# The first loads of a fused attention and token-mixing kernel: first k tile in four parts, second k tile cast by VectorE

## The chip, the cores and the metric

The kernel runs on one core of one Trainium2 chip. That core has a matrix engine (TensorE, PE in the profile), whose weight loads are shown apart (PEld), three engines for elementwise work (VectorE is DVE, ScalarE is ACT, GpSimd is POOL) and SyncE (SP), which here only issues DMAs. Each engine has its own list of instructions; they wait for one another by semaphores. The metric is the device time of the whole kernel in microseconds, the median of several runs; lower is better.

## What is computed

Sigmoid attention over 8 batches and 12 heads (sequence 448, head size 64), and then a token-mixing layer on its output:

```python
scores = (1/sqrt(64)) * q @ k.T - log(448)      # per batch and head
attn   = sigmoid(scores)
x      = (attn @ v), heads side by side         # 8 x 448 x 768
W_tok  = (1/8) * (x @ w_q) @ (x @ w_k).T        # 448 x 448 per batch
out    = relu(W_tok @ x) @ w_out
```

All inputs and the output are f32 in DRAM; the kernel casts to bf16 for TensorE.

## The kernel before: how the work is laid out

**Groups.** The work is cut into 24 groups (`quads`, L106): one batch and four heads each. A group has a q, a k and a v tile of 128 x 896 f32 (448 KB each, loaded by one DMA, `load1`, L155). For q and k each such tile is cast to bf16 (`cast1`, L173), transposed so that the head dimension lies on the partitions, and copied into a tile `qk[n]`. For groups 0 to 3 the transpose is done by TensorE into PSUM, with a copy from PSUM behind it (`tr`, L234, or `tr_part`, L755, for group 0); later groups use VectorE's own transpose.

**Scores.** Every group has seven score steps i = 0 to 6 (`scores`, L280): four matmuls of 64 x 448 take the i-th slice of k against all of q, into two PSUM banks, and ScalarE takes the sigmoid of the 128 x 896 result (L289). So there are 168 sigmoids. Then `values` (L295) multiplies with v. The rest, the token mixing of one batch, is spread among the scores of later groups.

**Order of the work.** Nothing is reordered by a compiler: instructions stand on each engine in the order in which the program emits them. That order is the hand-written string `PLAN` (L117): each letter is one step, in order. `S` is the next score step; `q` and `k` the transposes of the next group's q and k by TensorE; `p`/`P` a value step; `F` a filler matmul of zeros (L776); `K` the second part of group 0's k (L809). The plan of before starts `FFSSFKSFSSqFSkFSFSp`.

**Casts and loads.** `ORDER` (L657) lists the loads in their order: `q1 k1 v0 q2 .k2 v1 k3 ...`. Loads go through six buffers (`ring`, `pump_loads`, L679): a load is emitted when the cast of the tile six places earlier has been emitted, and waits for it. Names without a dot are cast by GpSimd as soon as `ready` (L692) allows (`pump`, L721). Names with a dot are cast by VectorE: `cast_by_others` (L740) is called after each score step, and `cast_one` (L730) emits the cast at VectorE's place of that moment, if at least `LAG` = 9 score steps have been emitted since the load was.

**Group 0.** Its q comes by one DMA and its k by two (slices 0 to 2, `KA`, 192 KB, and slices 3 to 6, `KB`, 256 KB; L637 to L639). The prelude casts q in two parts (VectorE and ScalarE), k in two parts (both GpSimd, L746), and calls `tr_part` for q's two parts and for `KA`; the part `KB` is transposed and copied at letter `K`, so ahead of the third score step. Group 1 has kind "a": its q is transposed at letter `q`, its k at letter `k`, and then one VectorE copy takes both from PSUM (L272, 128 x 1792).

**PSUM.** The eight banks are handed out as four pairs in turn (`bank2`, L72); a score step, a `tr_part`, or a group's q and k transposes hold one pair until the copy or sigmoid that reads it is done.

Of the kernel before, what the change touches and what calls it, by code (L numbers as in the profile page):

```python
# [17 lines left out]
def kernel(  # L18
# [17 lines left out]
    P = 128  # L36
# [47 lines left out]
    def release(fb):  # L84
        if isinstance(fb, int):
            free2.append(fb)
        elif (fb[0], 1 - fb[1]) in halves:
            halves.remove((fb[0], 1 - fb[1]))
            free2.append(fb[0])
        else:  # L90
            halves.append(fb)
# [18 lines left out]
    def xt(u, j):  # L110
# [4 lines left out]


    PLAN = (  # L117
        "FFSSFKSFSSqFSkFSFSpFSpSqpPpPSPSSkFSpPSFSSabSrPSPSPXSsPSPpPSp"
        "pPpSPSXSwwSSzWWXwWSPPpSPppNSPSqkSXSSpUSPSpMpSPpPSqkSSPSpPMSP"
        "PPPSSWWXSSwWWWSPpcPSdMpSPPPSXSNSxSqkSUSpPSMppSppPSOoSMSOOqSk"  # L120
        "SoOSMrPpSppPSPSPOoSSsSOzXOSCLlLSLSLLSpPPPPcpPSSdOOSOSCNxSOSc"
        "USPPSPdprPSPPSPPsPPPSpSOPSXoSxSzooSCMLlCSLllLSPcpPSPPPPSCSOd"
        "XSSOOoSMpcpSPPPPSPSONSMYOxSpPpSpSCoodSpPPSoOSxSUSLcldllSLLPS"
        "PpSPpcpPdSoSOMSoSOSXmMrPsSpPPSPoSpOSPoSoozxSoScOSSOOOSOdNSOS"
        "USPppSMPpppPPPSpLPlSLLeppSflLOomgcOMooNOSxSoOStoSSOooeSpPdPP"
        "oPSpSPooSOfSooSSgPOoMpppSPPPOmMOSOSOSLLLlLSLSOoSOxScoOxSoSOO"
        "NdPPSPPPPSSPoOSOSOSooSxoSOSTPpSPPSPppPPMPPypMpPlLMLLyLLIxiiN"
        "IIuiIMiImmIIIOooOOOOoOOoooooo"
    )
    PLAN = "".join(PLAN)  # L130
    KIND = ["a"] + [t for t in PLAN if t in "qacer"]
# [65 lines left out]
    def transposes(ps, t16, r):  # L197

        for x, i in enumerate(range(r.start, r.stop)):
            for g in range(2):  # L200
                for h in range(2):
                    nc.tensor.transpose(
                        ps[HALF[g], h, x * NP : (x + 1) * NP], t16[HALF[h], i, g, :],
                        ident16[HALF[h], HALF[h]],
                    )
# [28 lines left out]
    def tr(n, nm, kind):  # L234
        t = "qk".index(nm)
        if kind == "s":
            return
        if kind == "r":
            qk[n] = p_qk.tile([P, 2, 2, NI, NP], BF16, tag="qk", name="qk")
            w = pq[n].rearrange("p e t i d y -> p e (t i d y)").bitcast(F32)  # L240
            for e in range(2):
                nc.vector.transpose(out=qk[n][:, e].rearrange("p t i n -> p (t i n)").bitcast(F32), in_=w[:, e])
            return
        if kind in "cdef":
            assert n in arranged
            w = pq[n].rearrange("p e t i d y -> p e (t i d y)").bitcast(F32)[:, t]
            if t == 0:
                qk[n] = p_qk.tile([P, 2, 2, NI, NP], BF16, tag="qk", name="qk")
            nc.vector.transpose(out=qk[n][:, t].rearrange("p t i n -> p (t i n)").bitcast(F32), in_=w)  # L249
            if kind in "ef":  # L250
                if t == 0:
                    moves.append((n, p_mv.tile([P, 2, 2 * S], BF16, tag="mv", name="mv")))
                nc.vector.transpose(out=moves[-1][1][:, t].bitcast(F32), in_=w)
            return
        t16 = ld.pop((nm + "16", n))
        if t == 0:
            ps_qk[n] = bank2()
        fb, _, ps = ps_qk[n]
        if kind in "abh":
            transposes_whole(ps[:, t], t16, slice(0, NI))  # L260
        else:
            transposes(ps[:, :, t * S : (t + 1) * S], t16, slice(0, NI))
        if t == 1:
            qk[n] = p_qk.tile([P, 2, 2, NI, NP], BF16, tag="qk", name="qk")
            copy = COPY["s" if kind in "jh" else "v"]
            if kind in "abh":
                copy(
                    out=qk[n].rearrange("p h t i n -> p t i h n"),
                    in_=ps[:, :, 0 : 2 * S].rearrange("p t (i h n) -> p t i h n", i=NI, h=2),
                )  # L270
            else:
                copy(  # L272
                    out=qk[n].rearrange("p h t i n -> p t h (i n)"),
                    in_=ps[:, :, 0 : 2 * S].rearrange("p h (t x) -> p t h x", t=2),
                )
            release(fb)
# [376 lines left out]
    for t in wqks:  # L653
# [1 line left out]


    ORDER = (  # L657
# [71 lines left out]

    def cast_one(e):  # L730
        todo = BY[e]
        if not (todo and todo[0] in issued and done["S"] >= issued[todo[0]] + LAG and ready(*todo[0])):
            return False
        nm, n = todo.pop(0)
        assert e == "v" or nm in "vw" or KIND[n] in "qa"
        cast_now(nm, n, e)
        pump()
        return True

    def cast_by_others():  # L740
        while cast_one("s") or cast_one("v"):
            pass

    q016 = p_c16.tile([P, NI, 2, HD], BF16, tag="q16", name="q16")
    k016 = p_c16.tile([P, NI, 2, HD], BF16, tag="k16", name="k16")
    for t16, t32, r, e in ((q016, q0, IA, "v"), (q016, q0, IB, "s"), (k016, k0, KA, "g"), (k016, k0, KB, "g")):  # L746
        COPY[e](
            out=t16[:, r].rearrange("p i b d -> p b i d"),
            in_=t32[:, :, cols(r)].rearrange("p b (i d) -> p b i d", d=HD),
        )  # L750
    cast |= {("q", 0), ("k", 0)}
    pump_loads()
    qk[0] = p_qk.tile([P, 2, 2, NI, NP], BF16, tag="qk", name="qk")

    def tr_part(nm, t16, r, e):  # L755
# [7 lines left out]

    tr_part("q", q016, IA, "v")
    tr_part("q", q016, IB, "s")
    tr_part("k", k016, KA, "v")
    used |= {("q", 0), ("k", 0)}
    pump()

    ALIKE = dict(a="q", c="q", e="q", r="q", b="k", d="k", f="k", s="k", j="k", h="k", X="x", y="x", Y="x", g="g", z="z", L="W", l="W", T="U", t="U", I="O", i="O")  # L770
    done["q"] = done["k"] = 1
    quads_r = []

    for t in PLAN:
        if t == "F":
            nc.tensor.matmul(pairs[free2[0]][:, 0], zeros[:, 0:P], zeros, start=True, stop=True)  # L776
            continue
        kind = ALIKE.get(t, t if t in "qkx" else t.upper())
        c = done[kind]
        done[kind] += 1  # L780
        tail = done["S"] == N * NI
        if t == "S":
            scores(*divmod(c, NI))
            cast_by_others()
        elif kind == "P":
            n, i = divmod(c, NI)
            values(n, i, tail, "s" if t == "p" else "v")
            if i == NI - 1:
                used.add(("v", n))
                pump()  # L790
        elif kind in "qk":
            if t in "rs":
                quads_r.append(c) if t == "r" else None
                if t == "s":
                    quadrants(c, 0)
            tr(c, kind, t)
            if t in "df":
                used.add(("q", c))
            if t not in "cers":
                used.add((kind, c))  # L800
                pump()
        elif t == "g":
            move()
        elif t == "z":
            n = quads_r.pop(0)
            quadrants(n, 1)
            used.update({("q", n), ("k", n)})
            pump()
        elif t == "K":  # L809
            tr_part("k", k016, KB, "v")  # L810
        elif kind == "x":
            tr_x(c, tail, t in "XY", "s" if t in "yY" else "v")
        elif kind == "W":
            mlp_wqk(*divmod(c, NC), tail, t in "wl", t in "Ll")
        elif kind == "C":
            for y in range(2):
                nc.sync.dma_start(out=wout16[HALF[y], NC + c, :], in_=wout16[HALF[1 - y], c, :])
        elif kind == "N":
            mlp_wkn(c)
        elif kind == "U":  # L820
            (mlp_tmp_tiled if t in "Tt" else mlp_tmp)(c, t in "ut")
        elif kind == "M":
            u, x = divmod(c, NC // 2)
            mlp_mix(u, x, t == "m", tail)
            if x == NC // 2 - 1:
                if u // 2 in TW:
                    chunks.extend((u // 2, ((u % 2, i), (u % 2, 6 - i))) for i in range(3))
                    if u % 2:
                        chunks.append((u // 2, ((0, 3), (1, 3))))
                else:  # L830
                    chunks.extend((u // 2, m, -1) for m in (range(3, NI) if u % 2 else range(3)))
        elif kind == "O":
            if (opened or chunks)[0][0] in TW:
                out_pair(t == "o")
            elif t in "Ii":
                out_halves(t == "i")
            else:
                out_chunk(t == "o", tail)
# [29 lines left out]
```

## Time and profile before

| | |
|---|---|
| median of 3 runs (lowest, highest) | 191.03 us (190.49, 191.83) |
| the profiled execution's own time | 189.1 us |
| its span in the profile | 187.0 us |
| TensorE (PE) busy | 174.7 us, 93% |
| ScalarE (ACT) busy | 163.5 us, 87% |
| VectorE (DVE) busy | 138.8 us, 74% |
| GpSimd (POOL) busy | 107.7 us, 58% |
| HBM read and written | 35.78 MB, 11.01 MB |

The span is what the profile covers, from the first instruction to the last; the own time has 2.1 us around it. The median is that of other executions. Busy time on PE counts matmuls as they overlap in the array, so a PE that is 93% busy is not at 93% of its peak. A timeline line gives start and duration in us, the engine, the line of the kernel, the operation, what is written and read, and, in brackets, how long the engine stood idle before it and what ended that.

### The profile page before, as it was taken

Reading aid. Unit: us, or ns where it says so; the run is one execution under the profiler, and the core shown is the slowest. Engines: PE = TensorE matmul, PEld = TensorE weight load, DVE = VectorE, ACT = ScalarE, POOL = GpSimd, SP = SyncE. Lnnn points to the kernel's source line nnn. Section 1 sums busy time; section 2 is a strip of 40 time slices with the busy share of each in tenths; the row PEclk is TensorE's granted clock in tenths of the full one; section 3 lists DMA queues with packets and bytes.
Section 4 is the critical chain, followed back from the end, with each engine's and each line's share of the span. In section 5 each row is a group of like instructions: output and inputs, shape, how many; then the busy total and the mean of one; then the engine's idle time right before and its main releaser. Section 6 shows DMA issues by size and latency. Waiting matters only on the chain.

```text
span 187.0 us, 8500 instructions
## 1 busy us (share of the span) xinstructions
PE 174.7 (93%) x3645; PEld 115.4 (62%) x3648; DVE 138.8 (74%) x211; ACT 163.5 (87%) x210; POOL 107.7 (58%) x145
## 2 busy tenths in 40 slices
PE   7688899989999999999999999999999999999990
PEld 7234556554555554565555776767997989786650
DVE  3234597677878999989898999979868465797810
ACT  4599999999999989999999999998999989975120
POOL 1366698991976999999999884396032910010000
PEclk9999999999999999999999999999999999999998
DMA  5999999975599989999998996984898634603485
GB/s 170 345 341 366 323 368 330 393 271 186 182 307 404 384 284 276 361 337 340 296 278 274 311 407 240 291 282 128 231 348 292 170 96 89 156 23 85 102 238 168
DMA packets 26389, 48.97 MB, mean 262 GB/s; under 512 B 4080, under 2 KB 20208, under 8 KB 26352
## 3 DMA queue, kind: packets, MB, share of 16 engines
q1 hardware_dynamic: 25952, 47.65, 78.6%
q10 hardware_dynamic: 400, 0.79, 1.2%
q8 instruction: 28, 0.46, 1.0%
q14 instruction: 9, 0.07, 0.1%
HBM read 35.78 MB, written 11.01 MB: 250 GB/s over the span
## 4 chain that ended last, share of the span: by engine, by line
PE 69%; DVE 14%; ACT 6%; DMA 4%; issue 3%; SPq 1%; POOL 1%; ACTq 0%; DVEq 0%
PE banks L284 15%; PE banks L302 13%; PE banks L497 13%; PE banks L577 11%; ACT at L289 5%; DMA k<-in_k_dram 4%; DVE qk L218 4%; PE banks L534 3%; DVE xt L311 3%; PE banks L368 3%; PE banks L412 3%; PE banks L342 2%; PE banks L325 2%; DVE mx L440 2%; DVE qk L272 2%
## 5 line engine op out<-in xcount | busy, mean ns | idle before, releaser
L289 ACT ACTIVATE at<-banks 128x896 bf16<-128x896 f32 x168 | 141.5, 927 | 5.3 <-PE banks L284 4.0
L284 PE MATMUL banks<-qk 64*64 64x448 bf16 x672 | 63.1, 359 | 3.5 <-DVE qk L272 0.9
L302 PE MATMUL banks<-at,v 64*64 64x448 bf16 x672 | 46.6, 350 | 0.2
L284 PEld LDWEIGHTS <-qk 64*64 64x64 bf16 x672 | 25.8, 105 | 24.9 <-issue 14.8
L497 PE MATMUL banks<-wout,mx 64*64 64x384 bf16 x672 | 35.5, 323 | 0.1
L188 POOL CAST v<-v 128x896 bf16<-128x896 f32 x22 | 20.4, 931 | 14.1 <-DMA v<-in_v_dram 13.0
L302 PEld LDWEIGHTS <-v 64*64 64x64 bf16 x672 | 23.1, 106 | 7.8 <-issue 1.7
L497 PEld LDWEIGHTS <-mx 64*64 64x64 bf16 x672 | 24.7, 107 | 3.3
L311 DVE CAST xt<-banks 128x896 bf16<-128x896 f32 x20 | 21.6, 1085 | 4.5 <-PE banks L302 4.2
L440 DVE TENSOR_SCALAR mx<-banks 128x1024 bf16<-128x1024 f32 (+2 forms) x21 | 21.1, 1010 | 5.2 <-PE banks L464 3.0
L577 PE MATMUL banks<-wout,mx 128*128 128x384 bf16 (+1 forms) x138 | 24.7, 320 | 0.0
L577 PEld LDWEIGHTS <-mx 128*128 128x128 bf16 x138 | 11.9, 98 | 10.5 <-issue 4.7
L178 POOL CAST qk<-k 128x896 bf16<-128x896 f32 x11 | 13.4, 1218 | 7.8 <-DVE qk L249 5.2
L178 POOL CAST qk<-q 128x896 bf16<-128x896 f32 x13 | 16.0, 1228 | 2.7 <-DVE mx L440 1.5
L249 DVE STREAM_TRANSPOSE qk<-qk 128x448 f32<-128x448 f32 x24 | 14.9, 628 | 0.0
L377 POOL COPY wq<-wqk 64x448 bf16<-64x448 bf16 x6 | 3.3, 554 | 17.4 <-DVE wqk L376 17.1
L153 POOL COPY qk<-swap 32x448 uint32<-32x448 uint32 x20 | 12.1, 606 | 1.2
L506 DVE COPY o<-banks 128x768 f32<-128x768 f32 x9 | 8.6, 952 | 5.1 <-PE banks L497 5.1
L147 POOL COPY swap<-qk 32x448 uint32<-32x448 uint32 x20 | 11.1, 554 | 1.2
L150 POOL COPY qk<-qk 32x448 uint32<-32x448 uint32 x20 | 11.1, 554 | 1.2
L606 ACT COPY o<-banks 128x384 f32<-128x384 f32 x10 | 4.8, 485 | 7.1 <-PE banks L577 4.9
L218 DVE STREAM_TRANSPOSE qk<-qk 32x448 f32<-32x448 f32 x16 | 10.2, 636 | 0.4
(89 smaller groups left out, 227.3 us busy)
## 6 DMA issues: line engine op xcount, KB each, us to landing
q<-in_q_dram SPq DMA_DIRECT2D x24, 448.0 KB, 5.8
v<-in_v_dram SPq DMA_DIRECT2D x24, 448.0 KB, 6.5
k<-in_k_dram SPq DMA_DIRECT2D x23, 448.0 KB, 6.4
out_dram<-o SPq DMA_DIRECT2D x51, 192.0 KB, 4.3
w<-in_moe_w_out_dram SPq DMA_DIRECT2D x6, 384.0 KB, 4.0
wout<-wout SPq DMA_DIRECT2D x12, 96.0 KB, 7.1
out_dram<-o ACTq DMA_DIRECT2D x3, 192.0 KB, 3.2
qk<-mv SPq DMA_DIRECT2D x8, 56.0 KB, 3.9
```

Source lines behind the costliest of these rows:

```text
L153: eng.tensor_copy(out=w[lo, 1], in_=z[lo])
L178: COPY[e](out=f[:, :, "qk".index(nm)].rearrange("p e i d y -> p e y i d"), in_=ld.pop((nm, n)).rearrange("p (y i e d) -> p e y i d", y=2, ...
L188: COPY[e](out=t16.rearrange("p i b d -> p b i d"), in_=ld.pop((nm, n)).rearrange("p b (i d) -> p b i d", i=NI),)
L218: nc.vector.transpose(out=qk[n][other : other + 32, h].rearrange("p t i n -> p (t i n)").bitcast(F32), in_=w[own : own + 32, 1 - h],)
L249: nc.vector.transpose(out=qk[n][:, t].rearrange("p t i n -> p (t i n)").bitcast(F32), in_=w)
L284: nc.tensor.matmul(sc[HALF[h], g, 0:S], qk[n][HALF[g], h, 1, i, :], qk[n][HALF[g], h, 0].rearrange("p i n -> p (i n)"), start=True, stop=True,
L289: nc.scalar.activation(at, sc[:, :, 0:S], ACTF.Sigmoid, bias=attn_bias, scale=attn_scale)
L302: nc.tensor.matmul(ps[HALF[g], h, 0:S], ld["v16", n][HALF[h], i, g, :], ats[n, i][HALF[h], g, :], start=(i == 0), stop=(i == NI - 1),)
L311: COPY[eng](out=xt(u, j)[:, :, 0:S], in_=ps[:, :, 0:S])
L440: nc.vector.tensor_scalar(dst, ps, moe_scale, 0.0, ALU.mult, ALU.max)
L497: nc.tensor.matmul(ps[HALF[x], y, 0:NB], mx[HALF[y], u, b, 64 * (i - 3 * y) : 64 * (i - 3 * y) + 64], wout16[HALF[y], slot(y, b), x * NB : ...
L577: nc.tensor.matmul(ps, mxs[w][:, 2 * S * c + m * P : 2 * S * c + (m + 1) * P], wout16[:, c, w0:w1], start=(c == 0), stop=(c == NC - 1),)
```

## The change

The parts of the change, in the order of the code:

- `PLAN` starts with one `F` in place of two, and letter `k` of group 1 comes one score step later (behind score step 6 of group 0, where it was behind 5). The rest of the plan is the same.
- `tr` for group 1 copies its q from PSUM at letter `q` and its k at letter `k`, each by a VectorE copy of 128 x 896, in place of one copy of 128 x 1792.
- `ORDER` has `.k1` for `k1`: group 1's k is cast by VectorE. For groups 0 and 1 the `LAG` of 9 score steps is dropped, so that the cast is emitted after the first score step.
- Group 0's k is cast and transposed in four parts: K1 (slice 0), K2 (slices 1, 2), K3 (slices 3, 4), K4 (slices 5, 6). GpSimd casts K1, K2 and K4, VectorE casts K3. K1 and K2 are transposed and copied in the prelude; K3 and K4 at letter `K`. The two DMAs of group 0's k stay as they are.
- The first `pump_loads()` is called ahead of the prelude's casts, and again behind them.
- One more matmul of zeros (128 x 128) stands ahead of the plan.

```diff
-        "FFSSFKSFSSqFSkFSFSpFSpSqpPpPSPSSkFSpPSFSSabSrPSPSPXSsPSPpPSp"
+        "FSSFKSFSSqFSFSkFSpFSpSqpPpPSPSSkFSpPSFSSabSrPSPSPXSsPSPpPSpp"
...
+        if n == 1:
+            if t == 0:
+                qk[n] = p_qk.tile([P, 2, 2, NI, NP], BF16, tag="qk", name="qk")
+            nc.vector.tensor_copy(
+                out=qk[n][:, :, t].rearrange("p h i n -> p h (i n)"), in_=ps[:, :, t * S : (t + 1) * S],
+            )
+            if t == 1:
+                release(fb)
+            return
...
-        "q1 k1 v0 q2 .k2 v1 k3 q3 q4 k4 v2 w0 v3 k5 k6 q5 "
+        "q1 .k1 v0 q2 .k2 v1 k3 q3 q4 k4 v2 w0 v3 k5 k6 q5 "
...
-        if not (todo and todo[0] in issued and done["S"] >= issued[todo[0]] + LAG and ready(*todo[0])):
+        if not (todo and todo[0] in issued and done["S"] >= issued[todo[0]] + (LAG if todo[0][1] > 1 else 0) and ready(*todo[0])):
...
+    pump_loads()
     q016 = p_c16.tile([P, NI, 2, HD], BF16, tag="q16", name="q16")
     k016 = p_c16.tile([P, NI, 2, HD], BF16, tag="k16", name="k16")
-    for t16, t32, r, e in ((q016, q0, IA, "v"), (q016, q0, IB, "s"), (k016, k0, KA, "g"), (k016, k0, KB, "g")):
+    K1, K2, K3, K4 = slice(0, 1), slice(1, 3), slice(3, 5), slice(5, 7)
+    for t16, t32, r, e in (
+        (q016, q0, IA, "v"), (q016, q0, IB, "s"), (k016, k0, K1, "g"), (k016, k0, K2, "g"), (k016, k0, K4, "g"),
+    ):
...
-    cast |= {("q", 0), ("k", 0)}
-    pump_loads()
...
-    tr_part("k", k016, KA, "v")
+    tr_part("k", k016, K1, "v")
+    tr_part("k", k016, K2, "v")
+    COPY["v"](
+        out=k016[:, K3].rearrange("p i b d -> p b i d"), in_=k0[:, :, cols(K3)].rearrange("p b (i d) -> p b i d", d=HD),
+    )
+    cast |= {("q", 0), ("k", 0)}
+    pump_loads()
...
+    nc.tensor.matmul(pairs[free2[0]][:, 0, 0:P], zeros[:, 0:P], zeros[:, 0:P], start=True, stop=True)
...
         elif t == "K":
-            tr_part("k", k016, KB, "v")
+            tr_part("k", k016, K3, "v")
+            tr_part("k", k016, K4, "v")
```

More of the change, by code (lines that the diff above doesn't have):

```diff
@@ L117 @@
     PLAN = (
-        "FFSSFKSFSSqFSkFSFSpFSpSqpPpPSPSSkFSpPSFSSabSrPSPSPXSsPSPpPSp"
[L119 to L128, printed above, removed]
+        "FSSFSKFSSqFSFSkFSpFSpSqpPpPSPSSkFSpPSFSSabSrPSPSPXSsPSPpPSpp"
+        "PpSPSXSwwSSzWWXwWSPPpSPppNSPSqkSXSSpUSPSpMpSPpPSqkSSPSpPMSPP"
+        "PPSSWWXSSwWWWSPpcPSdMpSPPPSXSNSxSqkSUSpPSMppSppPSOoSMSOOqSkS"
+        "oOSMrPpSppPSPSPOoSSsSOzXOSCLlLSLSLLSpPPPPcpPSSdOOSOSCNxSOScU"
+        "SPPSPdprPSPPSPPsPPPSpSOPSXoSxSzooSCMLlCSLllLSPcpPSPPPPSCSOdX"
+        "SSOOoSMpcpSPPPPSPSONSMYOxSpPpSpSCoodSpPPSoOSxSUSLcldllSLLPSP"
+        "pSPpcpPdSoSOMSoSOSXmMrPsSpPPSPoSpOSPoSoozxSoScOSSOOOSOdNSOSU"
+        "SPppSMPpppPPPSpLPlSLLeppSflLOomgcOMooNOSxSoOStoSSOooeSpPdPPo"
+        "PSpSPooSOfSooSSgPOoMpppSPPPOmMOSOSOSLLLlLSLSOoSOxScoOxSoSOON"
+        "dPPSPPPPSSPoOSOSOSooSxoSOSTPpSPPSPppPPMPPypMpPlLMLLyLLIxiiNI"
+        "IuiIMiImmIIIOooOOOOoOOoooooo"
     )
```

## The prediction

> **What bounds the kernel now.** The change touches only what happens before the scores of group 1, so I asked first what the start is worth to the end, then what the start waits for. The busy time by stage comes first (columns: stage, its length, then busy us and instructions of each engine, granted clock, DMA share, GB/s):
>
> ```profile
> 4.30:6.70 2.40, 2.04 (x23) 0.83 (x21) 0.94 (x3) 0.78 (x3) 0.50 (x1) 1.00 0.97 276
> 6.70:9.00 2.30, 0.90 (x13) 0.53 (x10) 0.30 (x1) 1.72 (x3) 0.90 (x2) 1.00 1.04 389
> 9.00:14.00 5.00, 4.34 (x100) 1.90 (x101) 1.75 (x3) 5.00 (x7) 3.45 (x4) 1.00 0.98 345
> 14.00:56.00 42.00, 39.05 (x809) 21.82 (x809) 30.35 (x39) 41.86 (x52) 32.20 (x40) 1.00 0.89 303
> 56.00:100.00 44.00, 43.56 (x758) 24.17 (x754) 40.69 (x58) 42.82 (x55) 40.10 (x52) 1.00 0.99 329
> 100.00:168.00 68.00, 67.63 (x1761) 53.78 (x1764) 54.90 (x81) 64.44 (x82) 29.75 (x42) 1.00 0.71 221
> ```
>
> The fourth number of each stage is ACT: 41.86 of 42 us from 14 to 56. PE is 99% busy from 56 to 168. So ACT bounds up to 56 and PE, with ACT close behind, from there. ACT's timeline says it more sharply:
>
> ```profile
> 5.12 0.48 ACT L758 COPY qk<-banks 128x384 bf16<-128x384 bf16 x1 [0.57 <-PE banks L210]
> 6.65 1.73 ACT L289 ACTIVATE at<-banks 128x896 bf16<-128x896 f32 x2 [1.05 <-PE banks L284]
> 8.96 46.96 ACT L289 ACTIVATE at<-banks 128x896 bf16<-128x896 f32 x57 [0.58 <-PE banks L284]
> ```
>
> Sigmoids 0 and 1 start at 6.65, number 2 at 8.96, and then 57 run without a gap, 46.96/57 = 0.824 us each. Number 3 thus starts at 8.96 + 0.82 = 9.78, and group 1's first, number 7, at 13.08. Whatever makes one of these late moves the whole row to 55.9. What feeds them is seen on POOL, DVE and PE:
>
> ```profile
> 4.87 0.50 POOL L747 CAST k<-k 128x384 bf16<-128x384 f32 x1 [3.57 <-DMA k<-in_k_dram]
> 7.52 0.61 POOL L747 CAST k<-k 128x512 bf16<-128x512 f32 x1 [2.15 <-DMA k<-in_k_dram]
> 8.72 0.93 POOL L188 CAST q<-q 128x896 bf16<-128x896 f32 x1 [0.58 <-DMA q<-in_q_dram]
> 9.92 0.93 POOL L188 CAST k<-k 128x896 bf16<-128x896 f32 x1 [0.27 <-DMA k<-in_k_dram]
> ```
>
> ```profile
> 5.80 0.36 DVE L758 COPY qk<-banks 128x384 bf16<-128x384 bf16 x1 [0.43 <-PE banks L210]
> 8.70 0.42 DVE L758 COPY qk<-banks 128x512 bf16<-128x512 bf16 x1 [2.54 <-PE banks L210]
> 11.38 1.09 DVE L272 COPY qk<-banks 128x1792 bf16<-128x1792 bf16 x1 [2.26 <-PE banks L202]
> 13.47 0.63 DVE L188 CAST k<-k 128x896 bf16<-128x896 f32 x1 [0.99 <-DMA k<-in_k_dram]
> ```
>
> The loads arrive one after another: group 0's k in two parts (cast from 4.87 and 7.52), group 1's q (8.72) and k (9.92). POOL stands idle before each, so each cast starts as its data lands. The chain that ended last begins with that fourth load:
>
> ```profile
> 2.76 7.11 DMA k<-in_k_dram
> 9.87 0.05 issue
> 9.92 0.94 POOL k L188
> ...
> 11.38 1.10 DVE qk L272
> 12.49 0.04 issue
> 12.53 0.38 PE banks L284 x4
> ```
>
> k of group 1 lands at 9.87. In the whole chain DMA has only this 4%; behind 14 us it is all PE, DVE and ACT, and it runs through ACT's row of sigmoids again from 39 to 46 us. A delay of that row has nothing to absorb it.
>
> **The change part by part.**
>
> *First two scores.* POOL casts f32 to bf16 in 0.503 us for 384 columns, 0.613 for 512: so about 0.28 for 128 (K1) and 0.39 for 256 (K2), both from the data that lands at 4.87. K2 ends near 5.5, its two transposes near 5.83 and, at DVE's 0.286 for a PSUM copy of 128x256 bf16 (L403), its copy near 6.14. Score 0 needs only K1, and PE has one filler and a quarter ahead of it in place of two: it starts near 6.05 in place of 6.22, a gain of 0.15 to 0.25 us. It is worth nothing alone, since score 2 waits for the second k load at 7.47 and sigmoid 2 follows sigmoid 1 with a gap of 0.58 already.
>
> *Third score.* In the plan the letter K still stands ahead of the third S, before as after, so the third score does not pass the last parts. It gains otherwise: where POOL cast 512 columns in 0.61 us, DVE casts 256 of them (K3) in about 0.29 (DVE rows: 0.227 for 128, 0.426 for 512, 0.627 for 896) and POOL 256 (K4) in about 0.39, side by side. Both end by 7.91, not 8.13; transposes and four matmuls end near 8.55 and sigmoid 2 starts near 8.6 in place of 8.96. Gain 0.34 us, up to here. If the casts hindered each other until one had run after the other, 0.3 us of it would go; that decides nothing, by what follows.
>
> *The cast of group 1's k on VectorE.* This is what sets the end. After the first S of the plan the list of VectorE's casts is tried. Its first entry is now k1; its load is emitted, k0 counts as cast, and without the lag the cast is emitted there: on DVE behind the cast of K3, and ahead of letter K with the PSUM copies of K3 and K4. It waits for the load that lands at 9.87. Queued behind it on DVE: the copies of K3 and K4, then group 1's q copy. Who waits for them: score 3, which needs K3's copy, and on PE everything behind score 3 (score 4, q of group 1, scores 5 and 6); so ACT too. The copy that came at 8.70 comes now at 9.92 + 0.63 (the DVE cast of the same shape at 13.47) = 10.55. K3's copy at 0.29 gives 10.82 (consecutive DVE rows overlap by up to 0.08, so 10.75 to 10.84). Then 0.05 to the matmuls (12.48 to 12.53), and 0.44 from first matmul to sigmoid (8.52 to 8.96): sigmoid 3 starts at 11.28 (11.23 to 11.33), where it started at 9.78: **+1.5 us**. Sigmoid 2 then ends at 9.4 and ACT idles 1.9 us.
>
> That DVE does not start the copies first rests on its order. A row of POOL shows such holding: at 119.71 a cast of k starts after an idle 5.24 us that DVE ended, and a cast of v whose load was issued at 108.99 (median 6.5 us to landing, so about 115.5) starts only behind it, at 120.81. [...]
>
> *Group 1's q and k copied one by one.* Two DVE copies of 128x896 bf16 from PSUM, about 0.62 each (between 0.424 for 512 and 0.69 for 1024), in place of one of 1.09. From sigmoid 3 at 11.28: score 6 needs the PSUM pair of sigmoid 3 (free at 12.1), k's transposes run near 12.7 to 13.1, its copy to 13.75, score 7 to 14.2; sigmoid 7 is due at 11.28 + 4 x 0.824 = 14.58. Hidden with 0.3 us to spare, where before it was 0.1. Without that cover it would cost up to the 0.3 us of one sigmoid's gap; that is the fourth rival.
>
> *Loads and POOL.* SP's order is the same: q0, both k0 parts, q1, k1, v0, q2, k2, v1, k3, q3. k2's load left at 8.16 as POOL ended its cast; it can leave 0.2 earlier, q3's 0.3 earlier (k1's cast ends at 10.55, not 10.86). DMA is 97 to 104% busy from 4.3 to 14, so nothing lands sooner that matters; bounds 0 and -0.3, and I take 0, since ACT has no gap up to 55.9 that an earlier load could close. POOL loses 0.93 us of work and waits for v0 (lands near 11.1) as before: 0. The zero matmul and the filler less are about 0.06 and 0.2 us of PE beside waits: 0.
>
> *Sum.* Span 187.0 + 1.5 = 188.5; with the 2.1 us around it 190.6 for the profiled execution, which stood 1.0% under the median. On the median: 191.03 + 1.5 = **192.5 us**, 0.8% slower. The gains ahead (0.2 and 0.34) end in the idle time before sigmoid 3 and are not in the sum.
>
> **The rivals.**
>
> 1. *Not slower: k1's cast does not hold the copies* (it lies behind them, or they pass). Then sigmoid 2's 0.35 us stays, and score 7 is ready by 12.1 with k copied alone: 191.03 - 0.35 = 190.7. For it: DVE is idle 2.54 us before 8.70. Against: the order of emission as read above. It decides if the K3 copy starts before 9. Chance 0.08.
>
> 2. *The delay is absorbed later.* ACT has gaps of 0.2 to 0.57 us from 58 to 154, about 2.7 us in all. If they came from loads rather than PE's list, running 1.5 us later with loads on time would close two thirds: +0.4, 191.4. For it: POOL waits 13 us for v loads. Against: the gaps are put down to PE, and no load is in the chain there. Chance 0.12.
>
> 3. *TensorE loses its clock.* PE now stands still from about 8.7 to 10.8. The warm-up matmuls from 0.98 took 3.33/32 = 104 ns each, those of 4.52 (0.56 - 0.22)/6 = 57 ns: the start is at half speed. If the still stretch brought that back, the 2.1 us of PE work from score 3 to 7 (five scores at 0.19, two sets of transposes at 0.25, three fillers at 0.2) would double to 4.2 in 3.3 us: +0.9, 193.4. Against: PE was idle 1.37 us before 8.19 and its transposes then were fast. [...] Chance 0.10.
>
> 4. *Group 1's scores come late as well*, by the PSUM pairs' changed turn or k's later letter: 0.3 to 0.8 more, 193.1. Chance 0.10.
>
> **How the numbers follow.** The forecast has 0.60, own range 191.9 to 193.1 (the size between 1.4 and 1.6 and the scatter of medians; three runs spread over 1.34 us). Of the rest, the range 191.1 to 193.8 takes in the third and fourth rival and the upper half of the second, and leaves out about 0.2. About 1% is what a measurement can tell here: below 189.1 or above 192.94. Above: 0.2 of the forecast's 0.60 by scatter, 0.09 of the third, 0.06 of the fourth: 0.27. Below: 0.03 at most, from the first. Within: 0.70.
>
> **What would show it.** In the profile after: a DVE cast of 128x896 near 9.9 with an idle time that DMA k ended, copies of 128x256 only behind it, near 10.5; ACT idle 1.5 to 2 us before the fourth sigmoid, near 11.3; then a row of sigmoids without a gap to about 57.4. Sigmoid 2 near 8.6 would show the gain ahead. Copies of K3 before 9 us would sink the forecast; a row of sigmoids that starts 1.5 us late and an end that is not, the absence of absorption; matmuls of twice the duration at 11, the clock.

## The result, and the profile after

| | before | changed |
|---|---|---|
| median, 22 runs each (lowest, highest) | 189.78 us (188.11, 191.83) | 192.23 us (189.77, 195.36) |
| profiled execution, its span | 189.1 us, 187.0 us | 191.47 us, 189.5 us |
| ratio to before (95% interval) | | 1.0098 (1.0069 to 1.0128) |

The change makes the kernel slower by about 1%. The ratio leaves out executions that lie over 1.5% above the fastest of their kernel; of the changed kernel these are 9 of 22, and the experiments show that it makes most of them itself, so the plain medians (2.45 us, 1.3%) tell its loss better.

One line of the change is told wrongly above. The changed plan starts `FSSFSKFSSqFSFSkFSp`, not `FSSFKSFSSq...` as the diff shown above has it: the third S does stand ahead of K, and the prediction reasons from the wrong order. What follows from that is under the third score below.

ACT's timeline of the changed kernel, which answers to the row of 57 sigmoids from 8.96 before:

```profile
5.11 0.48 ACT L769 COPY qk<-banks 128x384 bf16<-128x384 bf16 x1 [0.57 <-PE banks L210]
6.22 2.54 ACT L298 ACTIVATE at<-banks 128x896 bf16<-128x896 f32 x3 [0.63 <-PE banks L293]
10.25 3.35 ACT L298 ACTIVATE at<-banks 128x896 bf16<-128x896 f32 x4 [1.49 <-PE banks L293]
14.06 0.92 ACT L298 ACTIVATE at<-banks 128x896 bf16<-128x896 f32 x1 [0.47 <-PE banks L293]
15.22 20.64 ACT L298 ACTIVATE at<-banks 128x896 bf16<-128x896 f32 x25 [0.24 <-PE banks L293]
```

Three sigmoids now run in one piece from 6.22, 1.1 us ahead of before at the third. Then ACT waits 1.49 us, and the fourth starts at 10.25, where it started at 9.77 before. Two more gaps follow, at 14.06 and 15.22. DVE's timeline shows the hold:

```profile
6.02 0.29 DVE L779 CAST k<-k 128x256 bf16<-128x256 f32 x1
8.93 0.63 DVE L188 CAST k<-k 128x896 bf16<-128x896 f32 x1 [2.61 <-DMA k<-in_k_dram]
9.47 0.48 DVE L769 COPY qk<-banks 128x256 bf16<-128x256 bf16 x2
10.70 0.62 DVE L266 COPY qk<-banks 128x896 bf16<-128x896 bf16 x1 [0.74 <-PE banks L202]
```

DVE has cast K3 at 6.3 and stands 2.61 us at the head of its list, at group 1's k, until that load lands. The copies of K3 and K4 (L769, 9.47) come only behind it, though their transposes ended near 7.5. The chain that ended last goes the same way, in order of time:

```profile
2.75 6.15 DMA k<-in_k_dram
8.90 0.02 issue
8.93 0.04 DVE k L188
8.96 0.51 issue
9.47 0.29 DVE qk L769
9.77 0.04 issue
9.81 0.57 PE banks L293 x8
```

The two later gaps have another cause. The busy time by stage, with the granted clock third from the right:

```profile
9.00:11.00 2.00, 1.19 (x41) 0.74 (x41) 1.26 (x4) 0.75 (x1) 0.83 (x1) 1.00 1.06 401
11.00:13.00 2.00, 2.00 (x38) 0.84 (x34) 0.57 (x2) 2.00 (x4) 1.04 (x2) 0.56 0.97 301
13.00:15.00 2.00, 1.81 (x14) 0.44 (x17) 0.90 (x2) 1.51 (x2) 0.97 (x1) 0.59 0.86 242
```

From 11.2 to 14.7 TensorE ran at half its clock; before, it had 1.00 in all of this. That is the third rival. PE's timeline shows its idle time in the hold, and two fillers of one shape and two scores of one shape, fast and then slow:

```profile
9.81 0.57 PE L293 MATMUL banks<-qk 64*64 64x448 bf16 x8 [1.44 <-DVE qk L769]
10.54 0.39 PE L794 MATMUL banks<-zeros 128*128 128x512 bf16 x1
10.86 0.38 PE L293 MATMUL banks<-qk 64*64 64x448 bf16 x4
11.21 0.59 PE L794 MATMUL banks<-zeros 128*128 128x512 bf16 x1
11.73 0.59 PE L293 MATMUL banks<-qk 64*64 64x448 bf16 x4
```

Comparing the starts of the 168 sigmoids one by one shows what becomes of the delay. The columns are the changed kernel's three profiles (the second and third are the runs a1 and a2 below) minus the first profile of before, in us:

| sigmoid | first | second | third |
|---|---|---|---|
| 2 | -1.12 | -0.81 | -0.77 |
| 3 | +0.48 | +1.14 | +1.03 |
| 6 | +0.49 | +1.15 | +1.04 |
| 8 | +1.43 | +1.25 | +1.14 |
| 14 | +1.41 | +1.23 | +1.12 |
| 56 | +1.54 | +1.38 | +1.24 |
| 112 | +1.56 | +1.93 | +1.25 |
| 161 | +2.46 | +2.76 | +2.21 |

In the second and third profile nearly all of the delay at sigmoid 14 is there at the third. In the first only 0.48 us is; another 0.94 comes between sigmoids 6 and 8, in the gaps of the half clock.

### The profile page after: what moved, and what is told of

Read it like the earlier page. It is cut to its first block, busy times and chain, and to the rows that moved or that the text cites. A ratio compares the mean times of both kernels' runs of the same rounds, so it can differ in the third digit from the quotient of the medians.

```text
span 189.5 us, 8509 instructions
## 1 busy us (share of the span) xinstructions
PE 177.0 (93%) x3648; PEld 115.9 (61%) x3648; DVE 139.5 (74%) x216; ACT 163.9 (87%) x210; POOL 107.4 (57%) x145
## 4 chain that ended last, share of the span: by engine, by line
PE 65%; ACT 12%; DVE 11%; issue 5%; DMA 3%; SPq 1%; ACTq 0%; DVEq 0%
PE banks L293 14%; PE banks L506 13%; PE banks L311 12%; ACT at L298 11%; PE banks L586 10%; DMA k<-in_k_dram 3%; PE banks L543 3%; DVE qk L218 3%; PE banks L377 3%; DVE mx L449 2%; PE banks L421 2%; PE banks L351 2%; DVE xt L320 2%; PE banks L461 1%; PE banks L334 1%
```

## The experiments

Three theories. H: the place of the k1 cast on VectorE, ahead of two copies that the scores wait for. C: PE's clock falls behind that hold. D: the loads landed about 1 us sooner in the changed kernel's profile (k of group 1 at 8.90, not 9.87) through the change, and the loss comes from the loads or the other parts. "Clock" below is an execution's mean granted clock. It also counts the half clock behind the last matmuls, which is 0 to 2.9 us of the span in the profiles here (1.70 in the first of before, 0.72 in the first of the changed kernel) and takes up to 0.008 off the mean; a fall of 3.41 us, as in the first profile of the changed kernel, takes off 0.009. By this estimate a clock under 0.99 tells of a fall, one of 0.992 or more of none, and 0.990 or 0.991 can be either.

**The changed kernel again (a1, a2).** No edit.

> The changed kernel once more, nothing edited: a second profile, and its times beside those of the kernel before on this chip. Theory H (the hold): the VectorE cast of group 1's k stands ahead of the PSUM copies of K3 and K4 and waits for its load, so ACT idles about 1.5 us before the fourth sigmoid again, in every execution. Theory C (the clock): behind that hold PE's granted clock falls to half for about 3.4 us; executions in which it falls are 1 to 2 us longer than those in which it does not, so the times scatter more than those of the kernel before (spans with a mean clock of 0.995 near 188, those under 0.99 near 190 or more). Theory D (the loads): the loads of k landed about 1 us earlier in the changed kernel's profile because of the change; then they do so again (second part of group 0's k cast by 6.1, group 1's k landing near 8.9). If that was the one execution's luck, they land elsewhere between 6 and 7.5 and between 8.9 and 9.9. Ratio to before 1.007 to 1.013.

Measured: 1.0143 (1.0089 to 1.0198), above the range that was given; six executions with clocks of 0.970 to 1.000, three of them under 0.99.

> The changed kernel once more, nothing edited, for a third profile of it. Theory H: the fourth sigmoid starts behind an idle time of 1.3 to 1.9 us that begins with VectorE's wait for group 1's k; the offset against the kernel before stays the same from sigmoid 14 to 112 within 0.3 us. Theory C: the granted clock may or may not fall to half between 9 and 15 us; where it falls, sigmoids 7 and 8 are another 0.5 to 1 us late. Late stretch: if it belongs to the later start, 0.4 to 1.9 us are lost again between sigmoids 119 and 150.

Measured: one run, 191.42 us, clock 0.992. ACT's timeline, first of a1, then of a2:

```profile
6.54 2.54 ACT L298 ACTIVATE at<-banks 128x896 bf16<-128x896 f32 x3 [0.54 <-PE banks L293]
10.91 24.78 ACT L298 ACTIVATE at<-banks 128x896 bf16<-128x896 f32 x30 [1.83 <-PE banks L293]
```

```profile
6.57 2.54 ACT L298 ACTIVATE at<-banks 128x896 bf16<-128x896 f32 x3 [0.48 <-PE banks L293]
10.79 24.77 ACT L298 ACTIVATE at<-banks 128x896 bf16<-128x896 f32 x30 [1.69 <-PE banks L293]
```

The hold is in all three profiles. The clock stayed at 1.00 in both of these, and the gaps at sigmoids 7 and 8 are missing, save 0.1 us. k landed near 9.57 and 9.46, not at 8.90.

**The kernel before again (b1).** No edit.

> The kernel before once more, nothing edited, for a second profile of it. Theory D (the loads land earlier because of the change): group 0's second k part is cast at 7.5 again and group 1's k at 9.9. If the landings only differ from execution to execution: elsewhere between 6 and 7.5 and between 8.9 and 9.9. Late stretch: the changed kernel's profiles lose another 0.4 to 1.9 us between sigmoids 119 and 150, put down to issue on PE. If that comes with the later start, it is missing here (sigmoids 119 to 150 as long as in the first profile, 38.7 us, within 0.2); if it is scatter, it can be here too.

POOL's timeline of b1:

```profile
7.17 0.62 POOL L747 CAST k<-k 128x512 bf16<-128x512 f32 x1 [1.99 <-DMA k<-in_k_dram]
9.17 0.94 POOL L188 CAST q<-q 128x896 bf16<-128x896 f32 x1 [1.38 <-DMA q<-in_q_dram]
10.35 0.94 POOL L188 CAST k<-k 128x896 bf16<-128x896 f32 x1 [0.25 <-DMA k<-in_k_dram]
```

The landings scatter by execution: the unchanged kernel had its k at 9.9 and at 10.3, e7 below, which has the same loads, at 8.9, and the seven profiles with the changed loads in this order had it between 8.9 and 9.6. Whether the change makes them land sooner is not shown by so few; the load itself was issued at 2.76 us in the first profile of before and at 2.75 in that of the changed kernel. That the loss comes from the loads falls with the runs below: e1 and e4 had k at 8.95 and 8.90 without the loss, e3 at 9.88 with it. b1 (one run, 191.79 us, span 189.7, as long as the changed kernel's) also lost 1.47 us between sigmoids 133 and 154 against the first profile of before, more than a2 (0.97) did; so the late part of the loss in the table, between sigmoids 112 and 161, is nothing that only the change makes.

**The cast behind the copies (e1).**

```diff
-        if not (todo and todo[0] in issued and done["S"] >= issued[todo[0]] + (LAG if todo[0][1] > 1 else 0) and ready(*todo[0])):
+        if not (todo and todo[0] in issued and done["S"] >= issued[todo[0]] + (LAG if todo[0][1] > 1 else 0) and ready(*todo[0]) and (todo[0][1] > 1 or done["K"])):
```

> The changed kernel with one condition more: group 1's k is cast by VectorE only once letter K has been emitted, so its cast stands behind the PSUM copies of K3 and K4. All else as changed. Theory H: the idle time before the fourth sigmoid goes; sigmoids 0 to 6 run without a gap from about 6.2 to 12.0, and the first one that waits is group 1's first, which needs k's landing (8.9 to 9.9) + cast 0.63 + transposes 0.45 + copy 0.62 + scores and sigmoid start 0.5, so 11.2 to 12.2 us; sigmoid 7 starts near 12.1 where it did at 13.08 before and 14.06 after: ratio to before 0.995 (0.992 to 0.999). Theory C: with no still stretch of PE from 8.3 to 9.8 the clock stays at 1.0 throughout the start; same sign. Theory D (the time is made by the loads or by the other parts, not by the place of the cast): ratio 1.005 to 1.012 as changed.

Measured: 1.0011 (0.998 to 1.0043), all 12 clocks 0.992 or more. DVE's and ACT's timelines of e1:

```profile
7.80 0.62 DVE L769 COPY qk<-banks 128x256 bf16<-128x256 bf16 x2 [1.00 <-PE banks L210]
8.97 0.63 DVE L188 CAST k<-k 128x896 bf16<-128x896 f32 x1 [0.55 <-DMA k<-in_k_dram]
```

```profile
6.78 27.34 ACT L298 ACTIVATE at<-banks 128x896 bf16<-128x896 f32 x33 [0.76 <-PE banks L293]
34.30 21.42 ACT L298 ACTIVATE at<-banks 128x896 bf16<-128x896 f32 x26 [0.18 <-ACT at L298]
```

The copies run at 7.80, the idle time before the fourth sigmoid is gone, and the row runs on to 34 us without a stop. The loss goes with the place of one instruction. The gain that was expected on top (0.995) was not to be had.

**The cast on GpSimd (e4).** `ORDER` has `k1` again; all else as changed.

> The changed kernel with group 1's k left to GpSimd (no dot in ORDER), so that VectorE's copies of K3 and K4 have no cast ahead of them; all other parts of the change stay (four k parts, third scores ahead of K3 and K4, q and k of group 1 copied one by one, the filler and k letter moved). Theory H: the loss goes, ratio to before 0.996 to 1.002, and within 0.004 of the kernel whose k1 cast stands behind letter K (1.001). If one of the other parts costs as well: ratio 1.004 or more.

Measured: 1.0012 (0.9974 to 1.0049), clocks 0.992 or more. DVE's and ACT's timelines of e4:

```profile
7.71 0.62 DVE L769 COPY qk<-banks 128x256 bf16<-128x256 bf16 x2 [1.16 <-PE banks L210]
```

```profile
6.68 27.34 ACT L298 ACTIVATE at<-banks 128x896 bf16<-128x896 f32 x33 [0.69 <-PE banks L293]
```

The same as e1: the other parts together cost nothing that shows, and gain nothing that shows.

**The cast alone (e3).** The kernel before with `.k1` and without the lag for groups 0 and 1.

> The kernel before with one part of the change alone: group 1's k cast by VectorE without the lag of nine score steps, so ahead of the PSUM copy of group 0's second k part (128x512). Everything else as before, the plan too. Theory H: that copy moves from 8.7 to k's landing + 0.63; the fourth sigmoid starts 1.5 to 1.8 us later than 9.78, ratio to before 1.006 to 1.010 without the clock, up to 1.015 where it falls as well (PE stands still about as long as in the changed kernel). If the other parts of the change made the loss: ratio 0.998 to 1.002.

Measured: 1.0106 (1.0051 to 1.016). DVE's and ACT's timelines of e3:

```profile
9.90 0.63 DVE L188 CAST k<-k 128x896 bf16<-128x896 f32 x1 [3.56 <-DMA k<-in_k_dram]
10.44 0.42 DVE L758 COPY qk<-banks 128x512 bf16<-128x512 bf16 x1
```

```profile
7.09 2.78 ACT L289 ACTIVATE at<-banks 128x896 bf16<-128x896 f32 x3 [1.15 <-PE banks L284]
11.35 46.16 ACT L289 ACTIVATE at<-banks 128x896 bf16<-128x896 f32 x56 [1.48 <-PE banks L284]
```

The copy that stood at 8.70 before stands at 10.44, and this part by itself makes a loss as large as the whole change. Three of its six executions had clocks under 0.99.

**Fillers in the hold (e2).**

```diff
-        "FSSFSKFSSqFSFSkFSpFSpSqpPpPSPSSkFSpPSFSSabSrPSPSPXSsPSPpPSpp"
+        "FSSFSKFFFFFFFFSSqFSFSkFSpFSpSqpPpPSPSSkFSpPSFSSabSrPSPSPXSsPSPpPSpp"
```

> The changed kernel with seven more filler matmuls (letter F, 128x512 of zeros, some 0.2 us each) in the plan behind letter K's filler, ahead of score 3: PE has about 1.4 us of work in the stretch where it stood still, and score 3 is not later, since it waits for VectorE anyway. Theory H alone (the hold is all the cost): nothing changes, ratio to before 1.007 to 1.012 as for the changed kernel. Theory C: the granted clock stays 1.0 from 9 to 15 us, the sigmoids from the fourth on run without gaps of 0.47 and 0.24, and the ratio falls to 1.001 to 1.006, with the executions closer together. Neither: the fillers delay score 3 and the ratio goes over 1.012.

Measured: 1.0087 (1.0049 to 1.0125), inside the range that was expected of H alone and above that of C, into which its interval reaches. PE's timeline and the stages of e2:

```profile
8.07 1.89 PE L794 MATMUL banks<-zeros 128*128 128x512 bf16 x8 [0.54 <-ACT at L298]
10.34 0.57 PE L293 MATMUL banks<-qk 64*64 64x448 bf16 x8 [0.38 <-DVE qk L769]
```

```profile
9.00:11.00 2.00, 1.62 (x41) 0.75 (x39) 1.02 (x3) 0.23 (x1) 0.61 (x2) 1.00 1.05 403
11.00:13.00 2.00, 1.97 (x56) 0.83 (x43) 0.88 (x2) 2.00 (x3) 1.53 (x2) 1.00 1.00 299
```

The fillers end at 9.96 and delay nothing. What they change is the clock: none of 12 executions fell under 0.992, where 17 of the changed kernel's 29 were under 0.99. So the falls come from PE's rest in the hold. The hold itself stays: e2's mean is 191.75 us, against 192.26 for all 29 executions of the changed kernel. The 0.5 us between them is what the fillers gave back, and with executions of e2 between 190.0 and 193.7 us it is a rough figure.

**No fillers, no hold (e7).** The kernel before without its ten F.

> The kernel before with all ten filler matmuls (letter F) left out of the plan, and nothing else: no wait is added, PE only has less to do between 5 and 20 us. It leaves out work whose result is not used. Theory C: with less activity the granted clock falls to half for 3.4 us in some executions (mean clock under 0.99, where all 23 of the kernel before had 0.99 or more), those are 0.5 to 2 us longer, and the ratio is 1.002 to 1.010. If the clock falls only behind a stretch in which PE stands still for more than 1.5 us: all clocks 0.99 or more, ratio 0.997 to 1.002.

Measured: 0.9992 (0.9954 to 1.003); 8 of 12 clocks under 0.99, and those executions took 189.75 us in the mean against 188.71 for the other four. The clock fell with no wait added, by the ten fillers less alone: the longest idle time that PE's timeline of e7 names between 4 and 20 us is 1.02 us (in an execution whose clock held). Its price of 1.0 us does not show against the kernel before; what offset it was not separated, and four executions are few.

**k loaded ahead of q (e10).** The changed kernel with `.k1 q1` at the head of `ORDER`.

> The changed kernel with group 1's k loaded ahead of its q (ORDER starts .k1 q1), nothing else: VectorE's cast still stands ahead of the copies of K3 and K4, but its load lands where q's did, about 1.2 us sooner (7.7 to 8.7). Theory H (the price is the wait for that load): the fourth sigmoid starts 1.35 us behind k's landing as in the four profiles of the hold (landing 8.90 to 9.56, start 10.25 to 10.91), so near 9.1 to 10.1, and its idle time falls from 1.5-1.8 to 0.3-0.8. q, now landing near 9.5, is cast by GpSimd to 10.4 and transposed ahead of score 5, so a second gap of 0.3 to 0.9 us can come before the sixth sigmoid. Ratio to before 1.002 to 1.008, below the changed kernel's. If the price were the VectorE work itself (one cast more) or the other parts of the change: ratio 1.010 as the changed kernel.

Measured: 1.0038 (0.9994 to 1.0082), for the seven executions with clocks of 0.994 or more. The other five had clocks of 0.968 to 0.982 and took 192.7 to 195.1 us, and over all 12 the median is 191.20 us, against 189.02 for the kernel before. So the early load does not keep the clock. DVE's and ACT's timelines of e10:

```profile
8.16 0.63 DVE L188 CAST k<-k 128x896 bf16<-128x896 f32 x1 [1.07 <-DMA k<-in_k_dram]
8.70 0.48 DVE L769 COPY qk<-banks 128x256 bf16<-128x256 bf16 x2
```

```profile
9.47 1.73 ACT L298 ACTIVATE at<-banks 128x896 bf16<-128x896 f32 x2 [0.58 <-PE banks L293]
11.47 1.73 ACT L298 ACTIVATE at<-banks 128x896 bf16<-128x896 f32 x2 [0.26 <-PE banks L293]
```

The load landed at 8.13, and the fourth sigmoid started at 9.47, 1.34 us behind it. From cast to sigmoid it is 1.31 or 1.32 us in all five profiles of this hold: 8.93 to 10.25, 9.59 to 10.91, 9.48 to 10.79, 9.45 to 10.77 (e2), 8.16 to 9.47. What the hold costs follows the landing. Behind q, which is now the later load, small gaps follow (0.26 us before the sixth sigmoid, where 0.3 to 0.9 was expected), and at sigmoid 14 the row is 0.49 us behind the first profile of before.

**No hold and few fillers (e8).** e1 with the six fillers behind the third left out (the expectation says seven).

> The changed kernel with the k1 cast behind letter K (as in the run whose ratio was 1.001) and seven of its nine fillers left out: those behind score 3 of group 0 on; two stay at the start with one behind K. It leaves out work whose result is not used. If a version can beat both kernels it is this one: the hold is gone, and PE has 1.4 us less to do. Theory: where the clock stays at 1.0, ratio 0.994 to 0.999. Against it, the clock: without fillers the kernel before fell under a mean clock of 0.99 in 8 of 12 executions, which were 1.0 us longer than its others; if that happens here too, ratio 0.997 to 1.003 with clocks of 0.98 to 0.99.

Measured: 1.0035 (1.0002 to 1.0069), one clock of 12 under 0.99. ACT's timeline of e8:

```profile
6.34 27.48 ACT L298 ACTIVATE at<-banks 128x896 bf16<-128x896 f32 x33 [0.63 <-PE banks L293]
34.00 21.42 ACT L298 ACTIVATE at<-banks 128x896 bf16<-128x896 f32 x26 [0.18 <-ACT at L298]
```

This row is the earliest of all, 0.9 us ahead of the first profile of before at sigmoid 14 and still 0.5 at 133, and the kernel is not faster; by the interval it is slightly slower. No version that beats the kernel before was found.

## Why the prediction was right, step by step

**The number.** Near, and partly by luck. The forecast added 1.5 us to 191.03, a median of three executions; 22 of them have 189.78, 1.25 us less, and from there the sum gives 191.3. The measured step is 2.45 us, 0.95 more than forecast. The base was too high and the step too small, and so 192.5 came within 0.3 us of 192.23.

**The hold.** Right in place and order, and in size from the cast on. The forecast put the fourth sigmoid 1.36 us behind the start of the cast (9.92 to 11.28); the profiles have 1.31 to 1.32. The start itself was carried over from one profile: 9.92, where the changed kernel's three profiles have 8.93, 9.59 and 9.48. So the fourth sigmoid was later by 0.48, 1.14 and 1.03 us, not 1.5; 1.5 less the earlier landing gives 0.53, 1.20 and 1.09. e3, whose k landed at 9.88 as in the first profile of before, has 1.58, with a copy that is larger by 0.1 us. As the landing scatters, also without the change (b1's row is 0.40 us behind the first profile's), this part of the sum is known no better than that. That DVE would not let the copies pass, on which the +1.5 us rests, was the author's estimate; no profile of before shows it. The changed kernel's profiles do: DVE stood idle for 2.61, 3.03 and 2.14 us ahead of group 1's cast, and the copies of K3 and K4 came only behind it.

**Carried to the end, not absorbed.** Right. From sigmoid 14 to 70 the offset moves by no more than 0.35 us in any of the three profiles, and the second rival did not happen. The 0.8 to 1.0 us that come on top between sigmoids 112 and 161 were in no sum, and b1 has more of them (1.47).

**The clock: the third rival, taken too small in its chance.** It had 0.10 and came in at least 17 of 29 executions of the changed kernel, against 1 of 69 runs of the kernel before beside these experiments. Its price was right for one fall: forecast 0.9, and 0.94 us in the first profile between sigmoids 6 and 8, where a1 and a2 lose 0.1. Between executions more shows. The 17 have a mean of 192.8 us. Nine with clocks of 0.992 or more have 191.0, and the three at 0.990 or 0.991, which can have had a fall, took 192.7 to 193.2. Nine of the 17 have clocks under 0.983, which is what one fall and the longest end of 2.9 us would leave, so by this estimate they fell for more than one stretch; no profile shows such an execution. That all of the 1.8 us between 192.8 and 191.0 is the clock's price is not shown, as the fillers of e2 gave back only 0.5. The step that failed is "Against: PE was idle 1.37 us before 8.19 and its transposes then were fast": that one stretch did not bring the clock down said little about a longer one, and e7 shows that no added wait is needed. The forecast's +1.5 is the price of the hold without the clock; the mean of those nine is 1.4 us above the mean of the 69 (189.6). This is close, though the three profiles put only 0.5 to 1.1 us of it at the hold; how much is the late scatter was not separated.

**The third score.** The step "the third score does not pass the last parts" was wrong, from the misread plan. Sigmoid 2 came 0.8 to 1.1 us earlier, not 0.34. It decided nothing, as the step said of its own gain: all of it ended in the idle time before sigmoid 3. K4's cast on GpSimd, beside K3's on VectorE, took 0.52 us, not 0.39.

**First two scores.** Forecast 0.15 to 0.25 us earlier; measured 0.43, 0.11 and 0.08. In the first profile full clock was first granted at 4.42 us, and PE's seven transposes of q took 0.56 us; ACT's idle time before its copy of them was 0.57, 0.94 and 0.94 us in the three profiles. The scatter goes with that.

**q and k copied one by one.** Said to be hidden with 0.3 us to spare. In a1 and a2 sigmoid 8 lost 0.1 us more: nearly hidden, and the fourth rival with its 0.3 to 0.8 us did not happen. In the first profile, at half clock, 0.47 and 0.24 us of gap showed.

**Loads.** k2's load was to leave 0.2 us earlier and left at 4.57, 3.6 us earlier, since it now takes the buffer of q0 rather than k0. Its cast came at 13.29 in place of 13.47, so this moved nothing.

**What stays open.** e1, e4, e7 and e8 start the row 0.3 to 0.9 us earlier than the first profile of before, and none is faster. Between sigmoids 112 and 161 every profile lost something else, from -0.3 to +1.9 us, the kernel before too; the waits of PE that come on top there have no reason named but "issue" (1.0 us in b1, 1.8 in e2). That scatter is larger than the gain sought, and its cause was not found.

## What to carry to other kernels

An instruction moved to another engine takes its wait with it (here 2.61 us on VectorE): before counting what it saves, list what stands behind it on the new engine and who waits for that, and give the new place the landing time of its data. A stall of an engine that feeds TensorE can cost twice, once by itself and once by the clock (0.48 and 0.94 us in the first profile of the changed kernel); look at the granted clock of several executions, not of one profile. A delay at the start of a kernel whose engines are full can arrive at the end whole, as here (1.41 us at sigmoid 14 and 1.56 at 112 in the same profile); that a gain of the same kind arrives too is not shown, since the row began up to 0.9 us earlier in e8 without a gain.

## What the runs showed of the hardware

How long PE rests does not by itself decide whether its clock falls. In the first profile of the changed kernel no gap of PE that its timeline names near the fall is over 1.44 us, and the clock went to half 1.4 us after work had begun again (9.81 to 11.24). The fall lasted 3.41 us, to 14.66. In a1, a2 and e3 the longest gap was longer (1.78, 1.6 and 1.69 us), and the clock held.

Nor does the busy time around the rest decide it by itself. Of the 3 us from 8 to 11, PE was busy for 1.56 in the first profile of the changed kernel, for 0.91 in a1 and for 1.12 in e3, and only the first has the fall. Full clock was granted without a break for 180.91 us in the first profile of before, and for 6.83 and 174.08 us, ahead of the fall and behind it, in that of the changed kernel; these are 53, 2 and 51 times the 3.413 us of the fall, to within 0.02 us. What sets the moment of a fall is not shown by these runs.
